# Single PSUM banks, projections in halves of 288 columns, conv stages in half chunks and a contiguous last-stage operand, in a two-branch kernel on one Trainium2 core

## The chip, the cores and the metric

The kernel runs on one core of a Trainium2 chip. The metric is the device time of one execution in microseconds; the median of a kernel's runs is quoted. Each ratio below is the mean time of one kernel's fast runs over the mean of the other's fast runs of the same rounds, so it is not quite the ratio of the medians quoted beside it. A run counts as slow when it is over 1.5% above the fastest of the same kernel; the ratios leave slow runs out, the medians do not. Profiles are of one execution each.

## The reference

Two independent branches of sequence length S = 2048 and width D = 576 are computed and concatenated.

```python
# branch A: short filter on k, product with v, long convolution by FFT, product with q
k_shift = sum of 4 shifted k * shift_k        # kernel: matmuls "cv"
kv = k_shift * v
y  = irfft(rfft(pad(kv)) * rfft(pad(ssm_k)))[:S] + kv * ssm_D
a  = q * y
# branch B: linear attention with 32 heads of 18
q, k, v = split(x @ wqkv)
pq, pk  = phi(q), phi(k)                      # phi: elu + 1
o  = (pq @ (pk^T v)) / (pq . sum(pk))
b  = o @ wo
out = concat(a, b)
```

## The kernel before

The kernel does the long convolution as transforms in stages on PE (two forward stages, a pointwise product, two inverse stages), for five chunks of channels: four of 128 and one of 64. Branch B is a chain of projections: `k`, the Gram-like product `g`, `q` and `o`. The two branches share no data, so their operations fill each other's waits.

The order is made in Python before anything is emitted: a planner holds every operation with its dependencies, an estimated duration per engine, its buffers and a rank (`key`), and picks repeatedly the operation that can start first. It also picks VectorE or ScalarE for each copy out of PSUM.

```python
class _Sched:
    PEN = 0.400000                            # extra cost of VectorE when an engine is picked
    def _slot(self, b, taken): ...            # the slot of b.cls that comes free first
sch = _Sched({'PS': 4, 'W8': NW8, ..., 'E1': 3, ...}, ...)
CLS = {'PS': ([128, 1024], FP32), ...}        # a PSUM slot is a pair of banks, four slots
TB0, TBS = 8.0, 1.450000                      # pace of branch B's ranks
TA0, TAP = 12.0, 24.000000                    # pace of branch A's ranks
```

A projection writes a whole row of 576 columns into a pair of banks, as 512 + 64:

```python
for n0, n1 in ((0, 512), (512, 576)):         # k; o likewise, g with 512 + 65
    for t in range(5):
        nc.tensor.matmul(ps.t[:, n0:n1], lhsT=xT[:, t, ...], rhs=wk[:, t, n0:n1], ...)
# one exponential (ScalarE) and one min/max (VectorE) over 576 columns
```

A conv chunk is transposed, exchanged by DMA and multiplied as a whole. The last stage reads the transposed operand in pieces:

```python
o_tv = op(k0(32), {'DVE': ...}, lambda e: nc.vector.transpose(     # 32x32 blocks of 4 bytes
    out=v4(Vt, dc, '').bitcast(FP32), in_=v4(V, dc, '').bitcast(FP32)), ev, (V, Vt))
...
vt = v4(Vt, dc, 'wrt')                        # [block w][row r][2 bf16]
nc.tensor.matmul(o, lhsT=Ere[:, b, :], rhs=vt[:, :, b, :], start=True, stop=False)
nc.tensor.matmul(o, lhsT=Eim[:, b, :], rhs=vt[:, :, 16 + b, :], start=False, stop=True)
```

For fixed row `r`, `vt[:, :, r, :]` is 64 pieces of 4 bytes, 128 bytes apart.

Of the kernel before, what the change touches and what calls it, by code (L numbers as in the profile page):

```python
# [16 lines left out]
D = 576  # L17
# [5 lines left out]
PAIRS = ((0, 1), (2, 3), (4,))  # L23
# [4 lines left out]
NW8, NW4, NP8 = 8, 5, 3  # L28
TB0, TBS = 8.0, 1.450000
TA0, TAP = 12.0, 24.000000  # L30
# [108 lines left out]
class _Buf:  # L139


    def __init__(self, cls, name):
        self.cls, self.name, self.users, self.t = cls, name, [], None
        self.slot, self.avail = None, 0.0


class _Op:
    def __init__(self, key, eng, fn, deps, bufs, dma):
        self.key, self.eng, self.fn, self.dma = key, eng, fn, dma
        self.deps = [d for d in deps if d is not None]  # L150
        self.bufs = bufs
        self.start = self.end = None
        for b in bufs:
            b.users.append(self)


class _Sched:
# [3 lines left out]
    PEN = 0.400000  # L161
    LAT = {'PE': 0.27, 'ACT': 0.12, 'DVE': 0.12, 'POOL': 0.15, 'SP': 0.0}

    def __init__(self, slots, free):
        self.ops = []
        self.slots = {c: [[0.0, None] for _ in range(n)] for c, n in slots.items()}
        self.free = dict(free)
        self.dma_free = 0.0
# [6 lines left out]
    def _slot(self, b, taken):  # L175
        best = None
        for i, (t, owner) in enumerate(self.slots[b.cls]):
            if (b.cls, i) in taken:
                continue
            if owner is not None:  # L180
                if any(u.end is None for u in owner.users):
                    continue
                t = max([u.end + self.LAT[u.on] for u in owner.users])
            if best is None or t < best[0]:
                best = (t, i)
        return best

    def run(self):
        left = list(self.ops)
        order = []  # L190
        while left:
            best = None
            for o in left:
# [3 lines left out]
                for b in o.bufs:  # L197
                    if b.slot is None:
                        s = self._slot(b, taken)
                        if s is None:  # L200
                            ok = False
                            break
                        ready = max(ready, s[0])
                        taken[(b.cls, s[1])] = (b, s[0])
                    ready = max(ready, b.avail)
# [26 lines left out]
            for (c, i), (b, t) in taken.items():  # L232
                self.slots[c][i][1] = b
                b.slot, b.avail = i, t
# [3 lines left out]
        for o in order:  # L238
            for b in o.bufs:
                if b.t is None:  # L240
                    b.t = self.make(b.cls, b.slot, b.name)
            o.fn(o.on)
        self.order = order
# [3 lines left out]
def kernel(  # L247
# [29 lines left out]
    sch = _Sched({'PS': 4, 'W8': NW8, 'W4': NW4, 'P8': NP8, 'E1': 3, 'DG': 2, 'X18': 2},  # L277
                 {'PE': 6.0, 'ACT': 9.5, 'DVE': 9.0, 'POOL': 8.0, 'SP': 0.8})
    CLS = {'PS': ([128, 1024], FP32), 'W8': ([128, 4096], BF), 'W4': ([128, S + 16], BF), 'P8': ([128, 4096], BF),
           'E1': ([128, 1024], BF), 'DG': ([128, 512], BF), 'X18': ([128, 16 * (D + 1)], BF)}  # L280

    def make(cls, slot, name):
        shape, dt = CLS[cls]
        return (psum if cls == 'PS' else work).tile(shape, dt, name=name, tag="%s_%d" % (cls, slot))[:]
# [41 lines left out]
    def evac(n):  # L326
        return {'ACT': 0.2 + n * 0.00078, 'DVE': 0.07 + n * 0.00104}
# [32 lines left out]
    for g in range(8):  # L360
        key = TB0 + g * 2.4 * TBS - 1.5
        ps = _Buf('PS', 'xT_ps')
# [16 lines left out]
    for g in range(4):  # L379
        for rr in range(4):  # L380
            r = 4 * g + rr
            key = kb(1.2)
# [3 lines left out]
            def mm(e, g=g, rr=rr, r=r, ps=ps):  # L386
                for n0, n1 in ((0, 512), (512, 576)):
                    for t in range(5):
                        nc.tensor.matmul(ps.t[:, n0:n1], lhsT=xT[:, t, r * 128:(r + 1) * 128], rhs=wk[:, t, n0:n1], start=(t == 0), stop=(t == 4))  # L389
            o1 = op(key, {'PE': 1.2}, mm, d_w + [o_xT[r // 2]], (ps,))  # L390
            o2 = op(key, {'ACT': 0.72}, lambda e, ps=ps, eb=eb: nc.scalar.activation(  # L391
                out=eb.t[:, 0:D], in_=ps.t[:, 0:D], func=ACT.Exp, bias=neg1[:]), [o1], (ps, eb))
            o3 = op(key, {'DVE': 0.72}, lambda e, ps=ps, eb=eb, r=r: nc.vector.scalar_tensor_tensor(  # L393
                out=xview(pb)[:, r, 0:D], in0=eb.t[:, 0:D], scalar=1.0, in1=ps.t[:, 0:D], op0=ALU.min, op1=ALU.max),
                [o2], (ps, eb, pb))
            st_pk.append(o3)
# [5 lines left out]
    for o in st_pk:  # L402
        o.deps.append(o_ones)
    o_gt = []
    for t in range(5):
        f0 = FT[t]
        ps = _Buf('PS', 'g_ps')
        last = None
        for pc in range(4):
            key = kb(0.97)  # L410

            def mm(e, pc=pc, ps=ps, f0=f0):
                for r in range(4 * pc, 4 * pc + 4):
                    for n0, n1 in ((0, 512), (512, 577)):
                        nc.tensor.matmul(ps.t[:, n0:n1], lhsT=xview(xb)[:, r, f0:f0 + 128],  # L415
                                         rhs=xview(pb)[:, r, n0:n1], start=(r == 0), stop=(r == 15))
            last = op(key, {'PE': 0.97}, mm, st_pk[4 * pc:4 * pc + 4] + d_x + [last, o_ones], (ps, xb, pb))
        xs = _Buf('E1', 'xs')

        def f(e, ps=ps, xs=xs):  # L420
            xs.f = xs.t[:, 0:2].bitcast(FP32)
            nc.vector.tensor_scalar(out=xs.f, in0=ps.t[:, D:D + 1], scalar1=EPS, scalar2=None, op0=ALU.mult)
        o2 = op(key, {'DVE': 0.1}, f, [last], (ps, xs))

        def f(e, ps=ps, xs=xs, t=t):
            if e == 'ACT':
                nc.scalar.activation(out=GT[:, t, :], in_=ps.t[:, 0:D], func=ACT.Identity, bias=xs.f)
            else:
                nc.vector.tensor_scalar(out=GT[:, t, :], in0=ps.t[:, 0:D], scalar1=xs.f[:, 0:1], scalar2=None,
                                        op0=ALU.add)  # L430
        o_gt.append(op(key, evac(D), f, [o2], (ps, xs)))
# [14 lines left out]
    for c, (h0, hn) in enumerate(HCH):  # L446
# [5 lines left out]
        out=wq[:, 0:4, :], in_=wqkv[0:512, 0:D].rearrange("(t p) n -> p t n", p=128)), st_pk),  # L452
        dma(tB[0] - 20, 0.08, lambda: nc.sync.dma_start(out=wq[64:128, 4, :], in_=wqkv[512:576, 0:D]), st_pk)]

    key = kb(0.9)
    ps = _Buf('PS', 'kv_ps')
# [7 lines left out]
    o1 = op(key, {'PE': 2.0}, f, o_gt + d_wv, (ps, wb))  # L464
# [7 lines left out]
    ps = _Buf('PS', 'z_ps')  # L472
# [22 lines left out]
    for c, (h0, hn) in enumerate(HCH):  # L495
        key = kb(0.27)
        ps = _Buf('PS', 'm_ps')
# [5 lines left out]
        o1 = op(key, {'PE': 0.27}, f, [o_kv] + d_wo, (ps, wb))  # L503
# [12 lines left out]
    def q_stage(g):  # L516
        o_ph = []
        for pair in PAIRS:
# [12 lines left out]
            o1 = op(key, {'PE': 1.07 * n}, mm, d_wq + o_xT[2 * g:2 * g + 2], (ps,))  # L531
# [20 lines left out]
        o1 = op(key, {'PE': 0.8}, f, o_ph + [o_z], (ps, rbuf))  # L552
# [17 lines left out]
        o3 = op(key, {'PE': 0.25}, f, [o2], (ps,))  # L570
# [3 lines left out]
        for pair in PAIRS:  # L574
# [19 lines left out]
    def out_stage(g, o_n):  # L594
        res = []
        for rr in range(4):
            r = 4 * g + rr
            key = kb(1.2)
            ps = _Buf('PS', 'o_ps')
            ob = _Buf('E1', 'ob')  # L600

            def f(e, ps=ps, rr=rr):
                for n0, n1 in ((0, 512), (512, 576)):
                    for c, (h0, hn) in enumerate(HCH):
                        nc.tensor.matmul(ps.t[:, n0:n1], lhsT=pqT(g)[0:hn, c, rr * 128:(rr + 1) * 128],  # L605
                                         rhs=wview(2)[0:hn, c, n0:n1], start=(c == 0), stop=(c == 4))
            o1 = op(key, {'PE': 1.2}, f, o_n + o_M, (ps, rbuf, wb))
            o2 = op(key, evac(D), lambda e, ps=ps, ob=ob: copy(e, ob.t[:, 0:D], ps.t[:, 0:D]), [o1], (ps, ob))
            dma(key, 0.15, lambda ob=ob, r=r: nc.sync.dma_start(
                out=outd[128 * r:128 * (r + 1), D:2 * D], in_=ob.t[:, 0:D]), [o2], (ob,))  # L610
            res.append(o1)
# [48 lines left out]
    def chunk(n, ci):  # L660
# [3 lines left out]
        k0 = lambda t: T + t * f * TAP / 30.0  # L664
# [25 lines left out]
        ps = _Buf('PS', 'hT_ps')  # L690
# [6 lines left out]
        o1 = op(k0(-4), {'PE': 0.95}, fn, [o_D, g1.get('s1h')], (ps, hb))  # L697
# [4 lines left out]
        def s1(key, src, sdep, which, wg=()):  # L702
            C = _Buf('W8', 'C' + which)
            ev = []
            for ri in range(2):
                for bg in range(2):
                    ps = _Buf('PS', 's1_ps')
# [8 lines left out]
                    o1 = op(key, {'PE': 0.45 if dc == 128 else 0.3}, fn, sdep[bg] + list(wg),  # L716
# [9 lines left out]
            o_t = op(key + 1, {'DVE': 0.07 + 2.1 * f}, lambda e: nc.vector.transpose(  # L726
                out=v4(Ct, dc, '').bitcast(FP32), in_=v4(C, dc, '').bitcast(FP32)), ev, (C, Ct))
            return Ct, o_t, ev

        def s2(key, Ct, o_t, which):  # L730
            T_ = _Buf('W8', 'T' + which)
            ev = []
            for c in range(nh):
                pss = [_Buf('PS', 's2_ps') for _ in range(2)]

                def fn(e, c=c, pss=pss):
                    for j in range(4):
                        n0 = (j * nh + c) * 512
# [4 lines left out]
                o1 = op(key, {'PE': 0.45}, fn, [o_t], (pss[0], pss[1], Ct))  # L743
                for ip in range(2):
                    def fn(e, c=c, ip=ip, ps=pss[ip]):
                        tv = T_.t[:, 0:32 * dc].rearrange("p (i n) -> p i n", i=4)
                        copy(e, tv[:, 2 * ip:2 * ip + 2, c * 512:(c + 1) * 512],
                             ps.t.rearrange("p (b n) -> p b n", n=512), (1.0 / 2048.0) if which == 'h' else 1.0)
                    ev.append(op(key + 0.5, evac(1024), fn, [o1], (pss[ip], T_)))
            return T_, ev  # L750
# [9 lines left out]
        for r in range(2):  # L760
            d_X.append(dma(k0(11), 0.26 * 2 * f, lambda r=r: nc.sync.dma_start(
# [118 lines left out]
```

## Time and profile before

| | before |
|---|---|
| time, median of 3 | 218.79 us (217.52 to 218.82) |
| span of the profiled run | 215.9 us |
| PE / VectorE / ScalarE busy | 183.4 / 164.9 / 121.0 us |
| span less PE busy | 32.5 us |

The first lines of the page of the kernel before: busy time by engine, then the busy share of PE and VectorE in 40 slices of the span, in tenths, and the clock granted to PE. DVE is VectorE, ACT ScalarE, PEld the weight load.

```profile
span 215.9 us, 5202 instructions
...
PE 183.4 (85%) x2277; PEld 123.6 (57%) x2277; DVE 164.9 (76%) x201; ACT 121.0 (56%) x137; POOL 15.8 (7%) x60
...
PE   0479998999999999998998989398988998887492
...
DVE  7926677797989486999677798958969779798800
...
PEclk9999999999999999999999999969999999995569
```

PE is busy nearly everywhere after the first 14 us, with gaps late, and its clock falls to about half near the end. The trace's clock records give 17.5 us at half clock, 13.7 of them from 195.0 us on. The line of the page that sums up the chain of work that ended last, by engine:

```profile
PE 58%; DVE 19%; ACT 8%; DMA 6%; issue 4%; SPq 2%; POOL 0%; ACTq 0%; DVEq 0%; POOLq 0%
```

The groups of instructions by line and form that the change touches, of the kernel before. Columns: line, engine, operation, output<-inputs, shapes, count | busy us, mean ns of one | idle us before them and what ended it.

```profile
L389 PE MATMUL k_ps<-w_k,xT 128*128 128x512 bf16 x80 | 22.2, 411 | 4.0 <-DVE xT L322 2.2 <-POOL xT L375 1.5 <-DVE Tu L322 0.2
...
L831 PE MATMUL is_ps<-Vt,Eim 128*128 128x128 bf16 x64 | 14.5, 288 | 0.0
...
L818 DVE STREAM_TRANSPOSE Vt<-V 128x2048 f32<-128x2048 f32 x4 | 9.2, 2311 | 0.4
...
L389 PE MATMUL k_ps<-w_k,xT 128*128 128x64 bf16 x80 | 5.3, 200 | 0.0
...
L714 PE MATMUL s_ps<-hT,Gre 128*128 128x128 bf16 x64 | 4.6, 219 | 0.8 <-DVE late_q L588 0.5 <-DVE u L782 0.3
...
L818 DVE STREAM_TRANSPOSE Vt<-V 128x1024 f32<-128x1024 f32 x1 | 1.2, 1245 | 0.1
```

Worked out from the start times in the trace, the median intervals of the kernel before are:

| matmul, columns | interval | matmul, columns | interval |
|---|---|---|---|
| k, q, o: 512 | 215 to 216 ns | k, o: 64 | 29 ns |
| g: 512 | 219 ns | g: 65 | 33 ns |
| conv stage `s_ps`: 128, contiguous | 56 ns | last stage: 128, in pieces of 4 bytes | 110 to 112 ns |

Busy time by stretch, of the kernel before (the stretch in us, its length, then us busy and instructions of each engine, the granted clock, DMA share and GB/s):

```profile
core 0: us, PE busy (x) PEld busy (x) DVE busy (x) ACT busy (x) POOL busy (x), PEclk, DMA share, GB/s
14.00:90.00 76.00, 74.02 (x937) 50.16 (x938) 56.57 (x67) 49.43 (x53) 2.63 (x11) 1.00 0.56 137
90.00:150.00 60.00, 52.49 (x645) 37.73 (x643) 50.24 (x63) 34.56 (x40) 0.49 (x3) 0.97 0.42 112
150.00:216.00 66.00, 52.64 (x676) 33.21 (x673) 47.39 (x45) 29.89 (x38) 0.00 (x0) 0.89 0.22 72
```

From 14 to 90 us PE is 97% busy (74.02 of 76.00). From 90 to 150 us PE has 52.49 of 60 us and VectorE 50.24, so each waits for the other.

### The profile page before, as it was taken

How to read it: one execution, taken by the hardware profiler on the slowest of the kernel's cores; microseconds unless marked ns; L12 is line 12 of the kernel's file. 1: busy time of each engine (PE TensorE's matmuls, PEld its weight loads, DVE VectorE, ACT ScalarE, POOL GpSimd, SP SyncE). 2: the span in 40 equal slices, each digit the busy share in tenths (PEclk: the TensorE clock that was granted, in tenths of full speed). 3: DMA queues.
4: the chain of work that ended last, by engine and by line, in shares of the span. 5: the costliest groups of instructions: out<-in, count | busy, mean ns of one | idle time of the engine just before them, and what ended most of it. 6: DMA issues, size and time to landing. Idle time of an engine off the chain costs nothing.

```text
span 215.9 us, 5202 instructions
## 1 busy us (share of the span) xinstructions
PE 183.4 (85%) x2277; PEld 123.6 (57%) x2277; DVE 164.9 (76%) x201; ACT 121.0 (56%) x137; POOL 15.8 (7%) x60
## 2 busy tenths in 40 slices
PE   0479998999999999998998989398988998887492
PEld 0326567755666865786865657155574674454340
DVE  7926677797989486999677798958969779798800
ACT  4556796869826253939296477028747448560122
POOL 8950101000000000100000000000000000000000
PEclk9999999999999999999999999969999999995569
DMA  6999997041910731196054703530000500410542
GB/s 201 351 293 255 207 259 169 24 173 24 265 37 0 197 146 52 23 305 118 0 162 84 291 3 97 85 76 0 32 27 29 225 3 0 155 58 28 167 79 84
DMA packets 42908, 25.82 MB, mean 120 GB/s; under 512 B 22916, under 2 KB 41604, under 8 KB 42372
## 3 DMA queue, kind: packets, MB, share of 16 engines
q1 hardware_dynamic: 42884, 25.47, 43.6%
q8 instruction: 18, 0.29, 0.5%
q14 instruction: 6, 0.05, 0.1%
HBM read 12.36 MB, written 4.72 MB: 79 GB/s over the span
## 4 chain that ended last, share of the span: by engine, by line
PE 58%; DVE 19%; ACT 8%; DMA 6%; issue 4%; SPq 2%; POOL 0%; ACTq 0%; DVEq 0%; POOLq 0%
PE g_ps L415 9%; PE q_ps L529 8%; PE o_ps L605 8%; PE k_ps L389 7%; PE cv_ps L775 7%; PE s_ps L714 5%; DMA x_sb<-in_B_x_dram 4%; PE is_ps L830 4%; PE is_ps L831 4%; PE s_ps L741 2%; DVE u L782 2%; ACT Th L320 2%; DMA X<-Th 2%; DVE Vt L818 2%; DVE Cth L726 2%
## 5 line engine op out<-in xcount | busy, mean ns | idle before, releaser
L605 PE MATMUL o_ps<-late_w,late_q 126*128 126x512 bf16 (+3 forms) x160 | 23.9, 305 | 5.3 <-DVE late_q L588 3.5
L389 PE MATMUL k_ps<-w_k,xT 128*128 128x512 bf16 (+1 forms) x160 | 23.2, 305 | 4.0 <-DVE xT L322 2.2
L529 PE MATMUL q_ps<-xT,w_k 128*126 128x512 bf16 (+1 forms) x100 | 24.9, 396 | 0.1
L320 ACT ACTIVATE ob<-o_ps 128x576 bf16<-128x576 f32 x16 | 10.4, 652 | 24.4 <-PE o_ps L605 11.2
L605 PEld LDWEIGHTS <-late_q 126*128 126x128 bf16 (+1 forms) x160 | 12.2, 102 | 18.9 <-issue 9.8
L415 PE MATMUL g_ps<-pk,x_sb 128*128 128x512 bf16 (+1 forms) x160 | 22.1, 287 | 0.1
L775 PEld LDWEIGHTS <-kT 128*128 128x128 bf16 x320 | 20.9, 153 | 1.6 <-issue 1.4
L775 PE MATMUL cv_ps<-dg,kT 128*128 128x128 bf16 (+1 forms) x320 | 21.5, 227 | 0.2
L389 PEld LDWEIGHTS <-xT 128*128 128x128 bf16 x160 | 11.4, 103 | 15.9 <-issue 2.9
L830 PE MATMUL is_ps<-Vt,Ere 128*128 128x128 bf16 (+1 forms) x80 | 16.3, 276 | 3.8 <-DVE Vt L818 3.0
L320 ACT ACTIVATE Th<-s_ps 128x1024 bf16<-128x1024 f32 x15 | 14.7, 1020 | 7.2 <-PE s_ps L741 7.2
L393 DVE SCALAR_TENSOR_TENSOR pk<-phi_k,k_ps 128x576 bf16<-128x576 bf16 x16 | 11.7, 746 | 8.7 <-ACT phi_k L391 8.7
L529 PEld LDWEIGHTS <-w_k 128*126 128x126 bf16 (+1 forms) x100 | 13.0, 138 | 8.4 <-issue 2.2
L320 ACT ACTIVATE Ch<-s_ps 128x1024 bf16<-128x1024 f32 (+1 forms) x16 | 15.1, 1016 | 4.3 <-PE s_ps L714 4.3
L320 ACT ACTIVATE Cu<-s_ps 128x1024 bf16<-128x1024 f32 (+1 forms) x15 | 13.2, 947 | 7.6 <-PE s_ps L714 7.6
L532 ACT ACTIVATE phi_q<-q_ps,neg_132 126x1024 bf16<-126x1024 f32 (+1 forms) x12 | 11.6, 970 | 10.2 <-PE q_ps L529 8.1
L320 ACT ACTIVATE V<-is_ps 128x1024 bf16<-128x1024 f32 x10 | 10.1, 1021 | 12.9 <-PE is_ps L807 12.8
L320 ACT ACTIVATE Tu<-s_ps 128x1024 bf16<-128x1024 f32 x12 | 11.9, 1022 | 8.3 <-PE s_ps L741 8.3
L831 PE MATMUL is_ps<-Vt,Eim 128*128 128x128 bf16 (+1 forms) x80 | 16.4, 277 | 0.0
L415 PEld LDWEIGHTS <-x_sb 128*128 128x128 bf16 x160 | 10.7, 98 | 9.3 <-issue 1.1
L837 DVE TENSOR_TENSOR q_p<-is_ps,q_p 128x1024 bf16<-128x1024 f32 (+1 forms) x10 | 11.2, 1118 | 6.2 <-PE is_ps L831 6.1
L391 ACT ACTIVATE phi_k<-k_ps,neg_132 128x576 bf16<-128x576 f32 x16 | 11.8, 741 | 5.1 <-PE k_ps L389 5.0
(127 smaller groups left out, 317.6 us busy)
## 6 DMA issues: line engine op xcount, KB each, us to landing
X<-Th SPq DMA_DIRECT2D x8, 512.0 KB, 3.6
h_sb<-in_A_ssm_k_dram SPq DMA_DIRECT2D x5, 512.0 KB, 4.5
x_sb<-in_B_x_dram SPq DMA_DIRECT2D x4, 576.0 KB, 7.6
out_dram<-ob SPq DMA_DIRECT2D x16, 144.0 KB, 1.9
v_p<-in_A_v_dram SPq DMA_DIRECT2D x2, 1024.0 KB
q_p<-in_A_q_dram SPq DMA_DIRECT2D x2, 1024.0 KB, 6.9
out_dram<-q_p SPq DMA_DIRECT2D x2, 1024.0 KB, 5.6
w_k<-in_B_wqkv_dram SPq DMA_DIRECT2D x2, 576.0 KB, 5.4
```

The costliest lines, as they stand in the source:

```text
L320: nc.scalar.activation(out=out_ap, in_=in_ap, func=ACT.Copy, scale=scale)
L389: nc.tensor.matmul(ps.t[:, n0:n1], lhsT=xT[:, t, r * 128:(r + 1) * 128], rhs=wk[:, t, n0:n1], start=(t == 0), stop=(t == 4))
L391: o2 = op(key, {'ACT': 0.72}, lambda e, ps=ps, eb=eb: nc.scalar.activation(out=eb.t[:, 0:D], in_=ps.t[:, 0:D], func=ACT.Exp, bias=neg1[:]) ...
L393: o3 = op(key, {'DVE': 0.72}, lambda e, ps=ps, eb=eb, r=r: nc.vector.scalar_tensor_tensor(out=xview(pb)[:, r, 0:D], in0=eb.t[:, 0:D], scal ...
L415: nc.tensor.matmul(ps.t[:, n0:n1], lhsT=xview(xb)[:, r, f0:f0 + 128], rhs=xview(pb)[:, r, n0:n1], start=(r == 0), stop=(r == 15))
L529: nc.tensor.matmul(ps.t[0:hn, 512 * j:512 * (j + 1)], lhsT=wq[:, t, h0:h0 + hn], rhs=xT[:, t, 512 * g:512 * (g + 1)], start=(t == 0), stop ...
L532: o2 = op(key, {'ACT': 0.2 + 0.4 * n}, lambda e, ps=ps, eb=eb, hn=hn, n=n: nc.scalar.activation(out=eb.t[0:hn, 0:512 * n], in_=ps.t[0:hn, ...
L605: nc.tensor.matmul(ps.t[:, n0:n1], lhsT=pqT(g)[0:hn, c, rr * 128:(rr + 1) * 128], rhs=wview(2)[0:hn, c, n0:n1], start=(c == 0), stop=(c == 4))
L775: nc.tensor.matmul(pv[:, bi, 0:dc], lhsT=kTb.t[:, c0:c0 + 16 * 127 + 1:16], rhs=dg[:, j, 0:dc], start=(j == 0), stop=(j == 3))
L830: nc.tensor.matmul(o, lhsT=Ere[:, b, :], rhs=vt[:, :, b, :], start=True, stop=False)
L831: nc.tensor.matmul(o, lhsT=Eim[:, b, :], rhs=vt[:, :, 16 + b, :], start=False, stop=True)
L837: nc.vector.tensor_tensor(out=qs, in0=pv[:, :, 0:dc], in1=qs, op=ALU.mult)
```

## The change

The intent is that PE and VectorE wait less for each other: PSUM is handed out in single banks (eight slots instead of four), the projections and their copies are cut to fit one bank (the conv stages still take two banks at a time), the conv stages work on half chunks so that one half can be multiplied while the other is copied, and the operand of the last stage is laid out in order. The planner's constants were set anew, and with them its estimates of some durations and its rule for which free slot to take. Cut to its core:

```diff
-PAIRS = ((0, 1), (2, 3), (4,))                       # q: one or two groups per PSUM tile
+SINGLES = ((0,), (1,), (2,), (3,), (4,))
-TB0, TBS = 8.0, 1.450000
-TA0, TAP = 12.0, 24.000000
+EVK, HK = 2.75, 1.0
+TB0, TBS = 8.0, 1.44
+TA0, TAP = 12.0, 24.83
 class _Op:
+        if any(x.cls == 'PS' for x in bufs) and 'PE' not in eng:
+            key -= EVK                               # copies out of PSUM rank earlier
-    PEN = 0.400000
+    PEN = 0.23
-    sch = _Sched({'PS': 4, ..., 'E1': 3, ...
+    sch = _Sched({'PS': 8, ..., 'E1': NE1, ...       # a tile takes n = 1 or 2 banks, NE1 = 5
...
+    HALF = ((0, 288), (288, 576))                    # k, g, o: one bank and one copy per half
-                for n0, n1 in ((0, 512), (512, 576)):
+        for n0, n1 in HALF:
...
-            o_t = op(key + 1, ..., lambda e: nc.vector.transpose(whole chunk), ev, (C, Ct))
+            for c in range(nh):                      # halves of 2048 columns
+                o_t.append(op(key + 1 + 0.1 * c, {'DVE': 1.15}, fn, ev, (C, Ct)))
...                                                   # likewise X<-Th by DMA, the products, V, Vt
-        nc.vector.transpose(out=v4(Vt, dc, '').bitcast(FP32), in_=v4(V, dc, '').bitcast(FP32))
+                vt = v4(Vt, dc, '').bitcast(FP32).rearrange("p (r w) -> p w r", r=32)
+                nc.vector.transpose(out=vt[:, 32 * c:32 * (c + 1), :], in_=V.t[...])
-                vt = v4(Vt, dc, 'wrt')
+                vt = v4(Vt, dc, '').rearrange("p (r d) -> p r d", r=32)
-                    nc.tensor.matmul(o, lhsT=Ere[:, b, :], rhs=vt[:, :, b, :], ...)
+                    nc.tensor.matmul(o, lhsT=Ere[:, b, :], rhs=vt[:, b, :], ...)
```

## The prediction

> **What bounds it now.** PE. The page gives PE 85% busy (183.4 us of 215.9), VectorE 165 us, ScalarE 121. The chain of waits is 58% PE, 19% VectorE, 8% ScalarE, 6% DMA. By stretches (table of windows): 14 to 90 us PE is 97% busy, so PE time removed there is time won; 90 to 180 us PE is busy 80.0 of 90 us and VectorE 75.2, so the two share the limit; 192 to 205 us PE waits for VectorE and runs at a granted clock of 0.61; the last 40 o matmuls take 6.94 us, where 20 took 2.62 us earlier.
>
> **What PE loses.** Start-to-start times from the timeline and chain:
> - Last stage: a 128-column matmul starts every 0.111 us (32 in 3.5 us). Its moving operand is read as 4-byte pieces 128 bytes apart. The contiguous s_ps matmuls of the same shape start every 0.056 us (8 in 0.45 us). The Trainium skill, "SBUF — State Buffer", section "Door 1: The DMA port swizzle", says each crossing to another 16-byte line pays a penalty; this trace agrees, twice the time. After: 0.056. Saves 4 chunks x 32 x 0.055 = 7.0 us, plus about 0.5 in the 64-column chunk.
> - Projections: a 512+64 pair costs 0.278 us (k), 0.271 (g), 0.262 (o). Scaling contiguous streaming (0.216 us per 512, q_ps), two of 288 take about 0.245. 80 pairs each: 2.7 + 2.2 + 1.5 = 6.4 us.
> Together 14 us of PE, about 6 to 7 of it in the stretch where PE alone limits.
>
> **What is added.** Fixed cost per instruction, from two sizes of one form: VectorE 0.12 to 0.14 us (1024 columns 1.205, 512 columns 0.664), ScalarE 0.18 (copy) to 0.26 (exponential). The order of instructions shows 201 VectorE instructions becoming 259 and 135 ScalarE ones becoming 174: about +8 us each, so VectorE near 173, ScalarE near 129.
>
> **What moves.** Eight single banks instead of four pairs let projection halves wait less for a free slot; half chunks let products, inverse stage and transpose of one half overlap the other. That shortens the latency chain behind 90 us, which I put at 2 to 4 us, but the added VectorE work takes most of it back there. The kernel now ends with the 64-column last stage, its multiply and the transfer out of q_p (3.2 us to landing before) instead of o with its short 1.9 us transfer: +1 to 2 us at the end, against fewer slow-clock o matmuls after a gap.
>
> **Sum.** -14 (PE) -3 (overlap) +4 (VectorE/ScalarE in the shared stretch) +1 (tail): about -12 us: 206.5 us, 80% range 200 to 213. Faster by over 2%: 0.88; within 2%: 0.10; slower: 0.02.
>
> **What would show it.** Last-stage matmuls starting every 0.056 us; k, g and o halves every 0.12 us; PE busy near 165 us or lower; VectorE busy 170 to 176 and the largest share of the chain grown from 19% towards 25 to 30%; g ending about 6 us earlier; transpose halves 1.25 us each.
>
> **What would make it wrong.** The transpose into Vt now writes 4-byte elements with a stride of 256 bytes; if that ran at half speed, VectorE would gain 10 us more and the time would be near 214. If VectorE's extra instructions all fall on the chain, half of PE's gain is lost. If the finer slots remove nearly all of PE's inner idle time, it goes to 200.

## The result, and the profile after

The changed kernel takes 199.92 us, median of 3 runs (199.06 to 200.05), against 218.79; the ratio of the fast runs is 0.9144, 95% interval 0.908 to 0.9207. The direction was right. The size was short: the point was 206.5 us, and the median lies 0.08 us under the low end of the stated range.

The page of the changed kernel, the same lines:

```profile
span 198.2 us, 5391 instructions
...
PE 171.6 (87%) x2277; PEld 130.2 (66%) x2277; DVE 174.9 (88%) x259; ACT 126.5 (64%) x176; POOL 15.8 (8%) x60
...
PE   0449999989999999999999999799986999869660
...
DVE  7943588999997997899999899999999999999880
...
PEclk9999999999999999999999999999999999985995
```

The span fell by 17.7 us: PE busy by 11.8 us (183.4 to 171.6, not to the 165 forecast) and the time in which PE is not busy by 5.9 us (32.5 to 26.6). Of the 11.8 us, 6.1 are the last stage (below) and up to 3 the clock: 11.5 us ran at half clock instead of 17.5, and where PE is busy a us at half clock does about half a us of work (the last-stage matmuls of the changed kernel start every 107 ns at half clock and every 56 ns at full). The rest is not accounted for. VectorE is busy 10.0 us longer (164.9 to 174.9) in a shorter span, 88% of it. The line of the chain:

```profile
DVE 2%; PE 2%; DVEq 0%; issue 0%
```

This chain could be followed back only over the last 14 us (its shares add up to 4%), so it says nothing on the rest of the span, and my forecast of VectorE's share of the chain cannot be read from it.

The groups of the changed kernel that answer to those shown before (`ps_all` is all of PSUM):

```profile
L408 PE MATMUL ps_all<-w_k,xT 128*128 128x288 bf16 x160 | 24.4, 313 | 4.6 <-DVE xT L341 2.2 <-POOL xT L394 2.1 <-DVE hT L341 0.3
...
L853 DVE STREAM_TRANSPOSE Vt<-V 128x1024 f32<-128x1024 f32 x9 | 18.0, 1995 | 0.2
...
L867 PE MATMUL ps_all<-Vt,Eim 128*128 128x128 bf16 x64 | 9.3, 243 | 0.0
...
L739 PE MATMUL ps_all<-hT,Gre 128*128 128x128 bf16 x64 | 4.6, 219 | 0.1
```

Three things are to be seen. The last-stage matmul is shorter (288 to 243 ns); by start times its interval is 56 ns instead of 110 to 112. The transposes into `Vt` take 1995 ns for 1024 columns where one of that size took 1245 before: writing in order of rows costs VectorE 18.0 us in all, against 9.2 + 1.2. And the `k` matmuls in halves take 24.4 us busy where the two old forms took 23.2 together (22.2 and 5.3, which overlap in time).

By stretch, of the changed kernel:

```profile
core 0: us, PE busy (x) PEld busy (x) DVE busy (x) ACT busy (x) POOL busy (x), PEclk, DMA share, GB/s
14.00:90.00 76.00, 75.07 (x970) 59.61 (x971) 64.62 (x98) 54.14 (x74) 2.80 (x11) 1.00 0.59 143
90.00:150.00 60.00, 55.89 (x734) 41.87 (x733) 58.63 (x90) 41.08 (x57) 0.11 (x1) 1.00 0.42 111
150.00:198.00 48.00, 37.19 (x550) 26.19 (x549) 40.93 (x46) 24.09 (x39) 0.00 (x0) 0.88 0.28 89
```

From 14 to 90 us PE was full before and is now (74.02, then 75.07 of 76 us), with VectorE 8 us busier. From 90 to 150 us VectorE is now busy 58.63 of 60 us instead of 50.24, and PE 55.89 instead of 52.49, with 734 matmuls instead of 645. Much of what was gained was gained in this stretch, where both engines used to wait.

### The profile page after: what moved, and what is told of

Read it like the earlier page. It is cut to its first block, busy times and chain, and to the rows that moved or that the text cites. A ratio compares the mean times of both kernels' runs of the same rounds, so it can differ in the third digit from the quotient of the medians.

```text
span 198.2 us, 5391 instructions
## 1 busy us (share of the span) xinstructions
PE 171.6 (87%) x2277; PEld 130.2 (66%) x2277; DVE 174.9 (88%) x259; ACT 126.5 (64%) x176; POOL 15.8 (8%) x60
## 5 line engine op out<-in xcount | busy, mean ns | idle before, releaser
L408 PE MATMUL ps_all<-w_k,xT 128*128 128x288 bf16 x160 | 24.4, 313 | 4.6 <-DVE xT L341 2.2
L552 PE MATMUL ps_all<-xT,w_k 128*126 128x512 bf16 (+1 forms) x100 | 24.2, 381 | 1.8 <-DVE late_q L611 1.6
L629 PE MATMUL ps_all<-late_w,late_q 126*128 126x288 bf16 (+1 forms) x160 | 23.0, 288 | 1.6 <-DVE late_q L611 1.6
L438 PE MATMUL ps_all<-pk,x_sb 128*128 128x288 bf16 (+1 forms) x160 | 22.2, 287 | 0.0
L806 PE MATMUL ps_all<-dg,kT 128*128 128x128 bf16 (+1 forms) x320 | 21.6, 226 | 0.7 <-DVE Tu L341 0.5
L339 ACT ACTIVATE Th<-ps_all 128x1024 bf16<-128x1024 f32 x14 | 13.8, 1021 | 9.2 <-PE ps_all L770 9.1
L411 ACT ACTIVATE phi_k<-ps_all,neg_133 128x288 bf16<-128x288 f32 x32 | 15.5, 501 | 5.8 <-PE ps_all L408 4.4
L853 DVE STREAM_TRANSPOSE Vt<-V 128x1024 f32<-128x1024 f32 x9 | 18.0, 1995 | 0.2
L339 ACT ACTIVATE Ch<-ps_all 128x1024 bf16<-128x1024 f32 (+1 forms) x15 | 14.4, 988 | 2.6 <-PE ps_all L739 2.6
L339 ACT ACTIVATE Cu<-ps_all 128x1024 bf16<-128x1024 f32 (+1 forms) x16 | 14.5, 950 | 1.0 <-PE ps_all L739 0.8
```

Of the source, the lines that this page charges most:

```text
L339: nc.scalar.activation(out=out_ap, in_=in_ap, func=ACT.Copy, scale=scale)
L408: nc.tensor.matmul(ps.t[:, 0:n1 - n0], lhsT=xT[:, t, r * 128:(r + 1) * 128], rhs=wk[:, t, n0:n1], start=(t == 0), stop=(t == 4))
L411: o2 = op(key, {'ACT': 0.46}, lambda e, ps=ps, eb=eb: nc.scalar.activation(out=eb.t[:, 0:288], in_=ps.t[:, 0:288], func=ACT.Exp, bias=neg1 ...
L438: nc.tensor.matmul(ps.t[:, 0:n1 - n0], lhsT=xview(xb)[:, r, f0:f0 + 128], rhs=xview(pb)[:, r, n0:n1], start=(r == 0), stop=(r == 15))
L552: nc.tensor.matmul(ps.t[0:hn, 512 * j:512 * (j + 1)], lhsT=wq[:, t, h0:h0 + hn], rhs=xT[:, t, 512 * g:512 * (g + 1)], start=(t == 0), stop ...
L629: nc.tensor.matmul(ps.t[:, 0:288], lhsT=pqT(g)[0:hn, c, rr * 128:(rr + 1) * 128], rhs=wview(2)[0:hn, c, n0:n1], start=(c == 0), stop=(c == 4))
```

## The experiments

Two questions were open: which part of the change brought the waits down, and why the size was missed. My theory after the result was that single banks and half chunks remove waits, and that the contiguous operand takes about 7 us from PE. The rivals: the new planner constants did it, or the new order of instructions is simply a lucky one.

All kernels gave correct results. Times are medians of all runs, with the ratio to the kernel before in the same rounds. In e1 two of four runs were slow, in e2, e3 and b1 one of four; the medians of their fast runs are 199.94, 208.25, 208.41 and 212.91 us. "Middle half" is worked out from each trace: every matmul is counted at a full-clock interval (216 ns for 512 columns, 123 for 288, 56 for 128, 29 for 64, 25 for 7 and fewer, 62 for the short filter, 81.5 for those of 32 rows, of which four take 326 ns; the same for all kernels), and the column gives the time from the point where a quarter of this work has been issued to the point where three quarters have. It leaves out the start and the tail. The choice of intervals matters: with 3 instead of 81.5 ns, for example, single entries move by up to 5.4 us. "Clock" is the mean, over the fast runs, of the span times what the granted clock falls short of 1. It is the most that PE can have lost to its clock.

```
run                        time us   ratio    middle half us   clock us
before                     218.79    -         95.7            6.9 to 7.2
changed                    199.92    0.9144    82.4            4.7
e1  old Vt layout          201.56    0.9193    84.8            2.0   (profile of a slow run)
e2  pairs of banks         208.92    0.9593    93.2            0.6   (profile of a slow run)
e3  whole chunks           208.50    0.9555    92.0            7.7
e4  old constants          209.12    0.9618    89.4            7.2
n1  pace -0.9%             207.59    0.9519    90.2            7.8
n2  pace +0.7%             204.33    0.9396    84.6            5.9
p1  full-row projections   205.95    0.9414    89.1            3.1
b1  before, new constants  214.14    0.9783    98.8            3.3
b2  before, 8-byte runs    211.75    0.9745    91.9            5.6
bn  before, pace +1%       211.52    0.9747    96.9            2.4
i1  changed, 8-byte runs   196.75    0.9053    82.0            3.1
```

In two of these traces (b2 and bn) 12 and 13 of the 2277 matmul records are missing, which moves their middle half slightly. The clock of the kernel before is that of its runs in the rounds of the experiments; the three runs in which it was timed beside the change have no clock on record.

### The layout of the last-stage operand undone (e1)

```diff
-                nc.vector.transpose(out=vt[:, 32 * c:32 * (c + 1), :], in_=...)   # in order of rows
+                nc.vector.transpose(out=Vt.t[:, hs].bitcast(FP32), in_=V.t[:, hs].bitcast(FP32))
-                    nc.tensor.matmul(o, lhsT=Ere[:, b, :], rhs=vt[:, b, :], ...)
+                    nc.tensor.matmul(o, lhsT=Ere[:, b, :], rhs=vt[:, :, b, :], ...)  # 4-byte pieces
```

> The changed kernel, but the operand of the last conv stage laid out as before: the transposes into Vt write contiguously, the last-stage matmuls read 4-byte pieces again. Last-stage matmuls should go back from 0.056 to 0.111 us each (PE +7 us) and a Vt transpose from 1.995 to about 1.22 us (VectorE -7 us). If PE alone bounds the changed kernel: 206 to 208 us. If VectorE bounds it: 193 to 196. If the two share the limit, as I think: 199 to 204.

Measured: 201.56 us, ratio 0.9193 (0.9134 to 0.9251), inside the 199 to 204 expected for a shared limit. The instruction order on all engines is the same as in the changed kernel (compared in the compiled programs), so nothing else differs. The instructions that touch `Vt`, in this run (count, then duration in ns as min/median/max):

```profile
L864 PE MATMUL ps_all<-Vt,Ere x80: 217/288/290, 71.3 to 195.3; 128*128 128x128 bf16 x64, 128*128 128x64 bf16 x16
L865 PE MATMUL ps_all<-Vt,Eim x80: 233/288/290, 71.4 to 195.3; 128*128 128x128 bf16 x64, 128*128 128x64 bf16 x16
L853 DVE STREAM_TRANSPOSE Vt<-V x9: 1200/1236/1246, 65.1 to 192.3; 128x1024 f32<-128x1024 f32 x9
```

The transpose is back at 1236 ns and the matmul at 288. So in the change the contiguous operand gives PE about 6 us (the intervals between last-stage matmuls add up to 15.4 us before and 9.3 after) and takes about 7 us of VectorE. Undoing both costs 0.5% (0.9193 against 0.9144), and the intervals overlap: in time, the contiguous operand, as it was done, is not shown to be worth anything (fast runs 199.74 and 200.13 us, against 199.06 to 200.05). But the fast runs of e1 had a clock of 0.99, those of the changed kernel 0.971 to 0.986, so up to 2.7 us (4.7 less 2.0) of a cost can be hidden.

### Pairs of banks, whole chunks, old constants (e2, e3, e4)

```diff
 # e2
-        self.cls, ..., self.n = cls, ..., n
+        self.cls, ..., self.n = cls, ..., 2 if cls == 'PS' else n
 # e3: one transpose, one exchange, one product per chunk, each waiting for both halves
-                o_t.append(op(key + 1 + 0.1 * c, {'DVE': 1.15}, fn, ev, (C, Ct)))
+            o_t = [op(key + 1, ..., transpose of the whole chunk, ev, (C, Ct))] * nh
 # e4
-EVK, HK = 2.75, 1.0 ... PEN = 0.23 ... TBS = 1.44 ... TAP = 24.83 ... / 30.0 * 1.01
+EVK, HK = 0.0, 1.0 ... PEN = 0.40 ... TBS = 1.45 ... TAP = 24.00 ... / 30.0
```

e3 also sets `HK`, the rank step between half chunks, to 0. e4 leaves the planner's new estimates of durations and its five instead of three `E1` buffers in place; no run undoes these.

> The changed kernel, but every PSUM tile takes a pair of banks (four slots, as before); instructions, halves and constants stay. If the finer slots gave most of the lost waits back (my theory): 206 to 212 us, with PE idle back near 28 us. If half chunks or the planner's constants did it: 199 to 202.

> The changed kernel, but the conv stages transpose, exchange and multiply whole chunks as before (one dependency for both halves), with banks, projections and contiguous operand kept. VectorE loses 16 instructions (about 2 us). If overlap between half chunks carries the gain: 204 to 208 us. If it does not: 197 to 201.

> The changed kernel with the scheduling constants of before (no early rank for evacuations, penalty of VectorE 0.40, pace 1.45 and 24.0). Instructions on chip are the same in kind and number, only their order and engine differ. Rival theory (the retuned planner made the gain): 206 to 214 us. Mine (banks and halves): 200 to 204.

Measured: 208.92, 208.50 and 209.12 us. In e2's profile, which is of a slow run, PE is not busy for 36.6 us (209.7 less 173.1), more than the 28 expected. Every one of the three looked like the cause, with 8.6 to 9.2 us each; together that would be 27 us out of 18.9. Either the parts work only together, or something else is common to the three. All three also make the planner produce another order, and no constant was tuned for that order. That called for a control.

### The control: the same kernel with another order (n1, n2, bn)

```diff
 # n1, from the changed kernel
-TA0, TAP = 12.0, 24.83
+TA0, TAP = 12.0, 24.60
 # n2, from the changed kernel
-TA0, TAP = 12.0, 24.83
+TA0, TAP = 12.0, 25.00
 # bn, from the kernel before
-TA0, TAP = 12.0, 24.000000
+TA0, TAP = 12.0, 24.240000
```

> Control for the planner: the changed kernel with one pace constant moved by 1% (24.83 to 24.60). Same instructions, but their order on PE and the choice of evacuating engine change in many places. If the losses of the earlier runs (7 to 10 us each) are only what any re-ordering costs: 205 us or more. If the changed kernel is not so delicate: 199 to 203 us.

> Second control for the planner on the changed kernel: pace 25.00 instead of 24.83 (0.7%). If 199.9 us is a picked schedule among schedules near 207: 204 to 209 us. If the first control was a bad draw: 199 to 202.

> The same control on the kernel before: pace 24.24 instead of 24.00 (1%). If the kernel before is as finely picked as the changed one: 222 to 228 us, and the change is then worth as much with either kind of schedule. If it is not: 214 to 220, and then several us of the difference between the two kernels are the picking.

Measured: 207.59, 204.33 and 211.52 us. A change of up to 1% in one rank constant, with the same structure, costs the changed kernel 4 to 8 us, and it *gains* the kernel before 2.5% (ratio 0.9747, interval 0.969 to 0.9803: a gain, though not surely one of 2%). I had expected the kernel before to lose or stay. The constant moves more than the order: the planner also picks another engine for some copies out of PSUM (VectorE has 258 and 262 instructions in n1 and n2, 259 in the changed kernel).

So the 199.92 us is a well picked order among orders near 204 to 208, while 218.79 is not the best time of the old structure. Of the old structure three orders were timed in ratios of 1, 0.9783 (b1, below) and 0.9747, mean 0.984; of the changed structure 0.9144, 0.9519, 0.9396, and with e4 0.9618, mean 0.942. The quotient, 0.957, says that structure is worth about 4% or 9 us, as an estimate from seven orders, which spread by 2.5% within the old structure and 4.7% within the changed one; the slowest of the changed structure (209.12 us) is still faster than the fastest of the old (211.52). By this estimate the rest of the 18.9 us comes from which order was picked. And the losses of e2, e3 and e4 in time are not clear of what a new order alone costs (n1 is at 207.59).

Does e2 or e3 stand apart from the controls in the middle half of the work? The controls of the changed kernel take 90.2 and 84.6 us for it. With pairs of banks (e2) it takes 93.2, nearer the kernels with pairs (95.7, 96.9, 98.8); whole chunks (e3) 92.0; old constants and full rows 89.4 and 89.1, between the controls. In e3, before and bn 3.4 us of it ran at half clock and in b1 6.8, which can have cost up to 1.7 us each and 3.4; in e2, n1 and n2 none. So e3 does not stand apart from n1, and e2 by 3 us. The stretch from 90 to 150 us of e2, all of it at full clock:

```profile
core 0: us, PE busy (x) PEld busy (x) DVE busy (x) ACT busy (x) POOL busy (x), PEclk, DMA share, GB/s
90.00:150.00 60.00, 52.93 (x711) 38.09 (x708) 55.50 (x77) 38.10 (x52) 0.74 (x3) 1.00 0.44 108
```

and of the control n1:

```profile
core 0: us, PE busy (x) PEld busy (x) DVE busy (x) ACT busy (x) POOL busy (x), PEclk, DMA share, GB/s
90.00:150.00 60.00, 54.93 (x690) 41.03 (x689) 56.68 (x90) 39.28 (x54) 0.11 (x1) 1.00 0.37 102
```

VectorE is busy 55.50 us in e2 and 56.68 in n1 (58.63 in the changed kernel, 50.24 before), PE 52.93 and 54.93, and e2 has more matmuls in it (711 against 690). This stretch alone does not settle it.

The clock tells them apart further. If "clock" is taken off the mean time of each kernel's fast runs, as an estimate that takes off the most that PE can have lost, the kernels with pairs come to 210.3 to 210.7 us (before), 210.2 (b1) and 209.6 (bn), and e2 to 208.0. The changed kernel comes to 195.0, its controls to 199.8 (n1) and 198.5 (n2), e3 to 200.3, e4 to 202.0 and p1, with pairs for `k`, `g` and `o`, to 202.4. So e2, which lost almost nothing to the clock and was still slow, lies with the kernels with pairs, and the single banks are the likely main part of the structure; e3 lies at the control n1. The gains of b1 and bn are about their smaller loss to the clock: with 13 records missing, bn still has the same work in 177.5 us of PE busy where the kernel before has 183.4. Whether an order brings its clock with it is not tested. All this is one order of e2 against several others, and an estimate; it is not shown beyond that.

### Full-row projections (p1)

```diff
-        for n0, n1 in HALF:                                    # k, o; g likewise
-            ps = _Buf('PS', 'k_ps')
+            ps = _Buf('PS', 'k_ps', 2)
+                for n0, n1 in ((0, 512), (512, 576)):
```

A version that also put `q` back into pairs could not be planned (the scratch slots ran out), so `q` stays in single banks here.

> The changed kernel with k, g and o projections in whole rows again (512+64 columns, pair of banks, one evacuation of 576 columns each); q stays in single banks, conv stages in halves, operand contiguous. PE streaming should not change (a 64-column matmul starts 0.029 us after its predecessor, so 512+64 costs 0.245 us and 2x288 costs 0.246), against the 6.4 us I had predicted; VectorE and ScalarE lose about 50 instructions. If halves of projections matter by finer waits: 204 to 209 us. If they do not: 197 to 201 us.

Measured: 205.95 us (ratio 0.9414), between the two controls. It falls in the range for "halves matter", but the controls do so too; halves of projections are not shown to matter in time. What is settled is PE's streaming: the matmuls of 288 and 289 columns start every 122 to 123 ns in the changed kernel, so two of them cost 245 to 246 ns, and 512 + 64 cost 215 + 29 = 244 to 245 before (252 for `g`).

### The constants alone in the kernel before (b1)

```diff
-    PEN = 0.400000
+    PEN = 0.23
-TB0, TBS = 8.0, 1.450000
-TA0, TAP = 12.0, 24.000000
+EVK = 2.75                               # used as in the change
+TB0, TBS = 8.0, 1.44
+TA0, TAP = 12.0, 24.83
```

> The kernel before with only the planner constants of the changed one (early rank of evacuations, penalty 0.23, pace 1.44 and 24.83). If the constants carry a gain by themselves: 208 to 213 us. If they help only together with banks and halves: 216 to 222 us.

Measured: 214.14 us, ratio 0.9783 (0.9681 to 0.9885, so a gain of 2% is not sure), in neither range. As bn shows that another constant alone gives as much, this is one more order of the old structure. The constants by themselves do not carry the gain.

### What a stride costs the transpose and the matmul (m1)

Appended after the last instruction of the changed kernel: the 128x1024 transpose with its output in runs of 1, 2, 4, 8, 16, 32 and 64 interleaved blocks, and last-stage-like matmuls that read such layouts.

```python
vt = xo[...].rearrange("p (a r w) -> p a w r", r=32, w=g)     # 4-byte elements written 4*g bytes apart
nc.vector.transpose(out=vt, in_=xin[...].rearrange("p (a w r) -> p a w r", r=32, w=g))
...
nc.tensor.matmul(o, lhsT=Ere[:, i, :], rhs=xo[...][:, :, i, :, :], ...)   # pieces of 4*g bytes
```

> The changed kernel with a bench appended after its last instruction (total time is not of interest): the 128x1024 transposes written with runs of 1, 2, 4, 8, 16, 32 and 64 blocks interleaved, and 128-column matmuls that read pieces of 4, 8, 16, 32, 64 bytes and one contiguous row. Ends should repeat the kernel: transpose 1.22 us contiguous, 1.95 to 2.0 us at strides of 128 and 256 bytes; matmul 0.111 us at 4 bytes, 0.056 contiguous. Rival readings: the transpose is slow for any stride (then no layout in between helps), or only for strides of 16 bytes and more; the matmul is slow only below 16-byte pieces.

The timeline of VectorE in this run, one line for each of g = 1, 2, 4, 8, 16, 32, 64 (start us, length us; from seven narrow windows):

```profile
193.54 1.25 DVE L894 STREAM_TRANSPOSE xo<-xin 128x1024 f32<-128x1024 f32 x1 [1.10 <-POOL xo L889]
194.81 1.25 DVE L903 STREAM_TRANSPOSE xo<-xin 128x1024 f32<-128x1024 f32 x1
196.09 1.98 DVE L903 STREAM_TRANSPOSE xo<-xin 128x1024 f32<-128x1024 f32 x1
198.11 2.02 DVE L903 STREAM_TRANSPOSE xo<-xin 128x1024 f32<-128x1024 f32 x1
200.16 1.89 DVE L903 STREAM_TRANSPOSE xo<-xin 128x1024 f32<-128x1024 f32 x1
202.09 1.91 DVE L900 STREAM_TRANSPOSE xo<-xin 128x1024 f32<-128x1024 f32 x1
204.03 1.90 DVE L897 STREAM_TRANSPOSE xo<-xin 128x1024 f32<-128x1024 f32 x1
```

Elements written 4 or 8 bytes apart: 1.25 us. From 16 bytes on: 1.89 to 2.02 us. The intervals of the matmuls, 16 of each layout, worked out from start times: 110 to 112 ns for pieces of 4 bytes, 55 to 57 ns for pieces of 8 bytes and for all larger ones. So there is one layout that costs neither engine anything measurable: pairs of blocks interleaved, g = 2. For the transpose the second rival was right: slow only from 16 bytes on. For the matmul the rival "slow only below 16-byte pieces" was wrong: pieces of 8 bytes are enough, which I had not expected.

### Runs of 8 bytes, in the changed kernel and in the kernel before (i1, b2)

```diff
-                vt = v4(Vt, dc, '').bitcast(FP32).rearrange("p (r w) -> p w r", r=32)
-                nc.vector.transpose(out=vt[:, 32 * c:32 * (c + 1), :], ...)
+                nc.vector.transpose(
+                    out=Vt.t[:, hs].bitcast(FP32).rearrange("p (a r w) -> p a w r", r=32, w=2),
+                    in_=V.t[:, hs].bitcast(FP32).rearrange("p (a w r) -> p a w r", r=32, w=2))
-                vt = v4(Vt, dc, '').rearrange("p (r d) -> p r d", r=32)
+                vt = v4(Vt, dc, '').rearrange("p (a r x) -> p a r x", r=32, x=4)
-                    nc.tensor.matmul(o, ..., rhs=vt[:, b, :], ...)
+                    nc.tensor.matmul(o, ..., rhs=vt[:, :, b, :], ...)
```

> The changed kernel with the operand of the last stage in runs of 8 bytes: pairs of blocks interleaved by the transpose, the matmul reads 8-byte pieces 256 bytes apart. Order of instructions on every engine is that of the changed kernel. The bench says transpose 1.25 us instead of 1.9 to 2.0 and matmul still 0.056: VectorE busy falls by 6 to 7 us to about 168, PE stays near 171. If VectorE shares the limit: 195 to 199 us. If PE and the clock alone bound it: 199 to 201.

> The kernel before with that operand layout alone; order of instructions on every engine is that of before, so no planner effect. PE loses about 7 us of last-stage streaming, VectorE nothing is added. If PE time removed is time won: 210 to 212 us. If PE only waits longer for VectorE and ScalarE: 215 to 217.

In both, the instruction order on every engine is the one of the kernel they were made from, so these two are free of the planner's effect, though not of the clock's.

i1 takes 196.75 us (196.52 to 197.41, five runs), ratio 0.9053 (0.9024 to 0.9082). It beats the kernel before, and all its runs are faster than all of the changed kernel's. Lines of its page (span and busy times), and two of the instructions on `Vt` (count, then duration in ns as min/median/max):

```profile
span 194.8 us, 5391 instructions
...
PE 170.1 (87%) x2277; PEld 128.6 (66%) x2277; DVE 169.0 (87%) x259; ACT 126.3 (65%) x176; POOL 15.8 (8%) x60
```

```profile
L866 PE MATMUL ps_all<-Vt,Ere x80: 190/217/229, 70.5 to 188.9; 128*128 128x128 bf16 x64, 128*128 128x64 bf16 x16
...
L853 DVE STREAM_TRANSPOSE Vt<-V x9: 1202/1237/1247, 64.3 to 186.8; 128x1024 f32<-128x1024 f32 x9
```

The transpose is at 1237 ns, the matmul as short as a contiguous one, and VectorE is busy 5.9 us less than in the changed kernel (174.9 to 169.0). The time fell by about 1% (0.9053 against 0.9144, from different rounds, whose intervals just touch), and up to 1.6 us of that can be the clock (4.7 less 3.1). VectorE time is thus worth at most a part of itself here, as expected for a shared limit.

b2 takes 211.75 us, ratio 0.9745 (0.9707 to 0.9783). With nothing added to VectorE, about 7 us of PE streaming (15.4 to 8.6 us of intervals) is worth 5.5 us of time, by the ratio 2.55% of 217. Up to 1.6 us of it can be the clock (7.2 less 5.6). Most of the PE time removed in the kernel before was time won.

## Why the prediction was right or wrong

**The limit: right, with a limit of its own.** PE was taken as the bound, VectorE as a near second after 90 us. b2 supports the first for the kernel before (7 us of PE gave 5.5 us, or about 4 without the clock). e1 and i1 agree with a shared limit in the changed one.

**"Saves 4 chunks x 32 x 0.055 = 7.0 us": right for PE, incomplete for the kernel.** The interval fell to 56 ns as forecast, worth 6.1 us over the two traces. The caveat that the strided transpose could cost VectorE 10 us came true at 7.5 us (`Vt` busy 10.5 to 18.0 us). I had left this cost out of the sum and only listed it as a risk. Undone together (e1), gain and cost nearly cancel in time. The half transposes forecast at 1.25 us each took 1.995.

**"80 pairs each: 2.7 + 2.2 + 1.5 = 6.4 us": wrong, the step that failed on PE.** I divided lengths of pieces of the chain by their count: 1.39 us for ten `k` matmuls, 2.17 us for sixteen of `g`. Such a piece contains the drain of its last matmul, and sometimes a wait. Start-to-start intervals in the same trace would have given 0.245 us for a 512 + 64 pair, and the two of 288 measure 0.246. The saving is nothing for `k` and `o`, and 80 x 6 ns = 0.5 us for `g`. The Trainium skill, "TensorE: Matmul & The Clock Gate", section "Wait — 56ns, not 53.3ns?", gives N / 2.4 GHz plus about 2.5 ns from the start of one matmul to the next at full clock; estimated from that, 512 columns take 215.8 ns, 64 take 29.2 and 288 take 122.5, so there is no difference. These traces agree to within a nanosecond (216, 29, 123). I had the page and did not put it against my reading.

**"About +8 us each" for VectorE and ScalarE: the VectorE total right, its parts off.** VectorE rose by 10.0 us to 174.9, in the stated 170 to 176. But 7.5 of it are the `Vt` transposes, and 4.8 us of copies of `V` went to ScalarE by the planner's choice, which leaves some 7 for the extra instructions. ScalarE rose by 5.5 us, to 126.5, not 129.

**"A latency chain ... 2 to 4 us, but the added VectorE work takes most of it back there": wrong, the second failed step and the larger.** In the stretch from 90 to 150 us VectorE went from 50.24 to 58.63 us busy, and PE with it from 52.49 to 55.89: the added work filled VectorE's waits. The time in which VectorE is not busy fell from 51.0 to 23.3 us (span less busy). The structure's part in the time is an estimated 9 us in all from seven orders, or about 11 with the clock taken off (210.1 less 198.8, the means of the same seven), and e2 points to the single banks for most of it. The prediction had named this case ("if the finer slots remove nearly all of PE's inner idle time, it goes to 200"); the time came, but PE was still not busy for 26.6 us.

**A term that was missing: the order itself.** The measured 199.92 us contains a picked order, worth 4 to 8 us against two neighbours (up to 3 of it the clock), and the 218.79 us an order that a 1% shift of one constant beats by 2.5%, about what it loses more to the clock. Of all terms this was the one that nothing in the diff or the profile before shows. That 206.5 came within 7 us is partly luck: 6 us too much was put on the projections, and the order and most of the overlap were left out.

**The tail: roughly right.** The kernel now ends with the 64-column last stage and its transfer out (3.7 us to landing). From the last matmul's start to the end it is 5.8 us, against 4.5 before: +1.3 us in the forecast +1 to 2. By the clock records in the traces, 11.5 us of the span ran at half clock instead of 17.5.

**"g ending about 6 us earlier": wrong.** The last `g` matmul starts at 86.4 us instead of 89.4, as the saving in the projections was not there.

What stays open: how the roughly 9 us divide between banks, half chunks and halves of projections. Each of e2, e3 and p1 changes the order too, and their times lie among the controls or within 1.5 us of them; only e2 stands apart once the clock is taken off. What brings the stretches at half clock is open as well.

## What to carry to other kernels

When a scheduler makes the order, run a control that changes its choices and nothing else before any part is given credit; here one constant moved by 1% or less changed the time by 2.5 to 4%, about the size of what undoing each part seemed to cost (3 to 5%). Then compare the granted clocks: here they differed by up to 0.035 between kernels, some 7 us. Experiments that keep the compiled order (a layout, a stride, an access pattern) give cleaner answers. Cost a stream of matmuls by the interval from start to start, never by the length of a busy piece over its count, and price both ends of a layout change: the engine that writes it as well as the one that reads it.

## What the Trainium skill lacked or had wrong

- "SBUF — State Buffer", section "Door 1: The DMA port swizzle", speaks of 16-byte lines and at least two hits per line for full speed. For VectorE's transpose the runs agree: 4-byte elements written 8 bytes apart 1.25 us, 16 bytes apart 1.98 us. For the moving operand of a matmul the figure needed is not there, and two elements in a line are not enough: bf16 pieces of 4 bytes run at 110 to 112 ns for 128 columns, pieces of 8 bytes at 55 to 57 ns, as contiguous ones.
- "VectorE: DVE Perf Modes", section "The three transpose paths", has no cost for a strided output of the 32x32 transpose: 1.25 us for 128x1024 contiguous, 1.89 to 2.02 us from 16 bytes on.
- "TensorE: Matmul & The Clock Gate", section "Wait — 56ns, not 53.3ns?", was right and enough on the split of the projections (216, 29 and 123 ns measured for 512, 64 and 288 columns).
- No page that I found says how far the order alone can move a kernel that is bound by several engines at once: 4.4 and 7.7 us of 200 here, with the same work and a few copies on another engine.
